# Attention, then two MoE blocks, on one core: all position-bias groups ahead of the attention loop, engines in hand-written order, and a full-height last key chunk

## The chip, the cores and the metric

The kernel runs as one program on 1 core of one Trainium2 chip. The metric is the device time of one execution in microseconds, as the median of several runs. The engines are TensorE (PE in the profile, PEld for its weight loads), VectorE (DVE), ScalarE (ACT), GpSimd (POOL) and SyncE (SP), which here only issues DMAs.

## The reference, cut to what matters

Attention with a learned position bias, then two feed-forward blocks. Everything is float32.

```
B, H, S, D = 4, 8, 576, 64
scores = q @ k.T / sqrt(D)
psi    = log1p(|i - j|) / log1p(max(i, 1))
bias   = relu(psi * w1 + b1) @ w2              # 32 hidden, then 8 heads
attn   = softmax(scores + bias[None])          # divided by (sum + 1e-9)
x      = attn @ v                              # 2304 tokens x 512
h = x @ w_in;  g = P(h) / (Q(h) + 1e-6);  x = g @ w_out        # 512 -> 2048 -> 512
h = max(x @ w1, x @ w2, x @ w3);          out = h @ w_out2     # 512 -> 768 -> 512
```

The bias depends on the two positions and the head only, so it is computed once for all four batches.

## The kernel before, in words

**Bias.** The 576 rows of the bias are cut into 36 groups of 16 rows: t = 0 to 3 with eight groups each, t = 4 with four. `bias_hidden` makes the hidden layer of one group in four tiles c = 0 to 3 of 128x576: c = 0 on ScalarE (L173), the others on VectorE (L176). `bias_out` multiplies them by w2 on TensorE (L185, PSUM tile `pb`), copies the result out as `bo` on ScalarE (L194; three of the 36 on VectorE, L192) and writes it to HBM with a DMA that ScalarE issues (L197). `bias_load` reads a finished block t back for a pair of heads, issued by SyncE (L204 to L212).

**Attention.** Heads go in pairs p, and a unit is (batch b, block t of 128 query rows, pair p); t = 4 has 64 rows for each of the two heads. There are 80 units, five for each of 16 pairs. In a tick n the loop body `attn_tick` issues the scores of unit n (`scores`, tiles `s`), the softmax of unit n (`reduce_min` on VectorE, `expo` on ScalarE), the reciprocal of unit n-1 (`normalise`: an addition on GpSimd at L269, a reciprocal on VectorE at L270, the broadcast `rb` on GpSimd at L272), the transposes of unit n-2 (`tp`, `tt`, where the last one at L303 transposes `rb`), and a part of a product with v (`attn_v`). `attn_v` runs over five chunks of keys: four of 128 keys as 128x64 tiles of TensorE for each head, and the last 64 keys of each head as a 64x64 tile (L338, `av<-att`). Before a pair can be scored, `split_kq` turns its k and q into high and low float32r parts in six pieces, all on GpSimd (L138 to L153); the loads for that are issued by SyncE ahead of time (`LL`, `SL` are the leads in ticks).

**The first ticks.** The first two pairs of batch 0 run interleaved. After each piece of their `split_kq` two bias groups are issued (`bias_step`), and the first 8 ticks (`NM0`) use the step list `A1`, which holds a bias group at four places. In this part a scheduler sets the order of all engines but SyncE. From tick 8 on the list is `A2`, and SyncE, TensorE and VectorE go in the order of the code (`MAN` 2), while the scheduler still places ScalarE and GpSimd.

**The end of attention.** Weights of the first feed-forward block are turned into high and low parts while the last 19 ticks run (`WT` 61; the low parts of w_in on GpSimd at L408), and x is read back and split from tick 72 on. Then `ffn_tick` and `moe_tick` follow, which the change leaves as they are.

**Buffers.** Most tiles (k, q, v, their parts, bias, `h`, `bo`, `e`, the weights) come from one pool `slot` of 35 buffers of equal size. A new tile takes the buffer of a released one and waits for the last reader of that one, whichever engine or DMA it is.

Of the kernel before, what the change touches and what calls it, by code (L numbers as in the profile page):

```python
# [8 lines left out]
F32 = mybir.dt.float32  # L9
# [20 lines left out]
KN = {'NSLOT': 35, 'NRAW': 3, 'NRAWX': 2, 'NATT': 4, 'HB': 0, 'NE': 'd', 'FP': 2, 'BL': 4, 'T4': 0, 'LSP': 1, 'KX': 4, 'HT': 'ss', 'EVP': 'da', 'TTP': 'dda', 'NXS': 4, 'EARLY': 0, 'NM0': 8, 'MAN': 2, 'MANF': 3, 'A1': ['b', 'T', 'sc', 'st', 'r0', 'av', 'b', 'b', 'b', 'sq', 'n', 'r1', 'p2', 'v0', 'v1', 'e0', 'e1'], 'A2': ['sc', 'av', 'p1', 'T', 'r1', 'r0', 'n', 'st', 'p2', 'sq', 'e0', 'e1', 'v0', 'v1'], 'LL': 10, 'SL': 4, 'LL0': 9, 'SL0': 4, 'SQ': [2, 1, 1], 'CUT2': 2, 'CUT3': 3, 'WS': 9, 'WE': 70, 'WT': 61, 'XT': 8, 'XA': 3, 'XB': 8, 'F': ['g2a', 'g2d', 'h', 'g1a', 'w', 'g2p', 'g1d', 'g1p', 'y', 'x', 'g3'], 'LOW': 4, 'LOM': 3, 'LOI': 0, 'GHI': 'dve', 'GLO': 'dve', 'BED': 8, 'BE0': 16, 'NU1': 'pool', 'XE': ['act', 'pool'], 'WR': 1, 'YSP': 'act', 'LAG': 2, 'EV1': 'dve', 'XSE': 'act', 'STQ': 'sp', 'PUQ': 'sp', 'NB0': 0, 'HP': 0, 'SB': 2, 'XLA': 3, 'XLB': 6, 'XSA': 11, 'YL': 10, 'YS': 14, 'WLOW': 1}  # L30
# [7 lines left out]
def tile_attention_moe(  # L38
# [67 lines left out]

    bias_d = [dr.tile([P if t < 4 else 64, H, S], F32, tag=f"bias{t}", name=f"bias_d{t}") for t in range(5)]
# [21 lines left out]
    def split_kq(b, p):  # L129
# [4 lines left out]
        lo_eng = pool  # L134
        low = slice(64, P)

        def q_hi():
            pool.tensor_scalar(qs, qr[:, :, :512], 1.0, 0.0, ALU.mult, ALU.add)  # L138

        def q_lo(u):  # L140
            lo_eng.tensor_tensor(qs[low, u], qr[low, u, :512], f32(qs[low, u]), ALU.subtract)

        def k_hi(u):
            pool.tensor_scalar(ks[u][:, 0], kr[:, u], 1.0, 0.0, ALU.mult, ALU.add)

        def k_lo(u):
            pool.tensor_tensor(ks[u][:, 1], kr[:, u], f32(ks[u][:, 0]), ALU.subtract)

        def tail(u):
# [4 lines left out]

        return [
            lambda: (q_hi(), k_hi(0)), lambda: (k_lo(0),), lambda: (q_lo(0), k_hi(1)),
            lambda: (k_lo(1),), lambda: (q_lo(1),), lambda: (tail(0), tail(1)),
# [5 lines left out]
    def bias_hidden(t, g):  # L163
        hs = []
        for c in range(4):
# [6 lines left out]
            if c == 0:  # L172
                act.activation(dst, src, AF.Relu, bias=bcol)  # L173
            else:
                on_pool = c == 3 and KN["HP"] and g % KN["HP"] == 0 and (t, g) >= (1, 4)
                (pool if on_pool else dve).tensor_scalar(dst, src, bcol, 0.0, ALU.add, ALU.max)  # L176
# [3 lines left out]
    def bias_out(t, g):  # L180
# [10 lines left out]
        if g % KN["BED"] == 1 and 8 * t + g >= KN["BE0"]:  # L191
            dve.tensor_scalar(bo, pb[:, :, :HS], sc, None, ALU.mult)  # L192
        else:
            act.activation(bo, pb[:, :, :HS], AF.Copy, scale=sc)  # L194
        rows = bias_d[t][g * 16:(g + 1) * 16].rearrange("i h j -> (i h) j")
        bo = bo.rearrange("p x j -> p (x j)")
        act.dma_start(rows, bo)  # L197
# [67 lines left out]

    def normalise(b, t, p):
        et, st = ex[b, t, p]
        r = st[:, 2:4] if t < 4 else st[:, 2:3]
        pool.tensor_scalar(r, r, 1e-9, 0.0, ALU.add, ALU.add)  # L269
# [53 lines left out]
    def attn_v(b, ts, p, js=range(5)):  # L323
# [279 lines left out]
    bnext = [0]  # L603

    def bias_step():
        i = bnext[0]
        if i < len(bgroups):
            if i == 0:
                bias_hidden(*bgroups[0])
            if i + 1 < len(bgroups):  # L610
                bias_hidden(*bgroups[i + 1])
            t, g = bgroups[i]
            bias_out(t, g)
            if g == (7 if t < 4 else 3):
                for p in range(NP):
# [274 lines left out]
```

## Time and profile before

| | us |
|---|---|
| median of 3 runs | 1082.96 (1081.78 to 1083.26) |
| the profiled execution, its own time | 1085.02 |
| its span, first to last instruction | 1083.2 |
| TensorE busy | 1034.7 |
| VectorE, ScalarE, GpSimd busy | 657.7, 622.8, 452.7 |

Busy times are over the whole span; the stages differ. Up to about 100 us the bias is made, attention runs to about 360 us, the first feed-forward block to about 790 us, the second to the end. The granted TensorE clock is 0.982 of full speed on the mean.

### The profile page before, as it was taken

To read this page: it belongs to the slowest core of one execution; us is meant where nothing else is said; L and a number is where in the kernel's file an instruction comes from. 1 tells how busy PE (TensorE), PEld (TensorE's weight loads), DVE (VectorE), ACT (ScalarE), POOL (GpSimd) and SP (SyncE) were. 2 spreads that over 40 slices of the span, in tenths; PEclk is the share of its full clock that TensorE was granted. 3 is DMA by queue.
4 is the path that set the end of the run, shared out by engine and by line. 5 is a ranking of instruction groups with operands and counts; after the bars stand their busy time and mean duration, and the time that the engine had idled before them with its cause. 6 is when DMAs were issued, how large, how long until landed. Compare 5 with 4: busy or idle time off the path is not lost. (4 is left out here: it accounts for less than half of the span.)

```text
span 1083.2 us, 16519 instructions
## 1 busy us (share of the span) xinstructions
PE 1034.7 (96%) x5996; PEld 814.2 (75%) x5996; DVE 657.7 (61%) x1296; ACT 622.8 (57%) x1226; POOL 452.7 (42%) x569
## 2 busy tenths in 40 slices
PE   5689899999998889999999999999999999999998
PEld 2247777777765668878889888788888888888887
DVE  8485667676665789777779877799954211111111
ACT  5685676776776878676678766788733211211111
POOL 7605767677696534332233322333533330211111
PEclk9799999999998889999999999999999999999999
DMA  7486854454453442010020200034243200201010
GB/s 266 138 298 216 294 182 151 158 190 158 157 184 123 147 142 78 1 59 1 0 79 1 79 1 0 24 114 136 84 142 105 78 1 1 78 1 59 1 40 20
DMA packets 43394, 107.94 MB, mean 100 GB/s; under 512 B 4784, under 2 KB 11184, under 8 KB 43312
## 3 DMA queue, kind: packets, MB, share of 16 engines
q1 hardware_dynamic: 38128, 96.27, 26.8%
q10 hardware_dynamic: 5184, 10.62, 2.5%
q8 instruction: 47, 0.77, 0.3%
q14 instruction: 35, 0.29, 0.1%
HBM read 77.90 MB, written 28.97 MB: 99 GB/s over the span
## 5 line engine op out<-in xcount | busy, mean ns | idle before, releaser
L454 PE MATMUL p<-ys,wm 128*128 128x512 f32 (+1 forms) x1080 | 227.0, 368 | 0.0
L454 PE MATMUL ph<-xs,wwi 128*128 128x512 f32 (+1 forms) x960 | 215.9, 373 | 3.5 <-ACT at L743 2.6
L454 PEld LDWEIGHTS p<-ys,wm 128*128 128x128 f32 x1080 | 188.9, 188 | 34.3
L454 PE MATMUL y<-gs,wwo 128*128 128x512 f32 (+1 forms) x905 | 204.4, 373 | 1.3 <-POOL gs L502 1.1
L454 PEld LDWEIGHTS ph<-xs,wwi 128*128 128x128 f32 x960 | 169.7, 190 | 38.4 <-POOL xs L446 3.0
L502 POOL TENSOR_TENSOR gs<-g,gs 128x512 fp32r<-128x512 f32 (+1 forms) x80 | 96.1, 1201 | 237.2 <-ACT gs L501 170.2
L454 PEld LDWEIGHTS y<-gs,wwo 128*128 128x128 f32 x905 | 158.4, 188 | 34.5 <-POOL gs L502 2.4
L264 ACT ACTIVATE e<-e,st 128x576 f32<-128x576 f32 x144 | 111.1, 772 | 61.2 <-DVE st L258 44.3
L258 DVE CUSTOM_DVE_ANT_0 e<-s,bias 128x576 f32<-128x576 f32 x144 | 104.3, 754 | 44.9 <-PE s L233 32.4
L546 POOL TENSOR_TENSOR h2s<-mx,h2s 128x512 fp32r<-128x512 f32 (+1 forms) x30 | 35.5, 1183 | 225.5 <-ACT h2s L545 225.5
L542 DVE TENSOR_TENSOR mx<-p,mx 128x512 f32<-128x512 f32 (+1 forms) x30 | 19.1, 637 | 141.4 <-PE p L454 137.5
L475 ACT ACTIVATE s<-ph,keep 128x512 f32<-128x512 f32 (+1 forms) x80 | 49.5, 618 | 90.3 <-PE ph L454 89.9
L545 ACT CAST h2s<-mx 128x512 fp32r<-128x512 f32 (+1 forms) x30 | 17.3, 578 | 127.8 <-DVE mx L543 127.8
L296 PEld LDWEIGHTS tp<-ident,e 128*128 128x128 f32 x576 | 62.1, 141 | 35.7 <-issue 20.1
L233 PE MATMUL s<-k,qs 128*128 128x288 f32 x512 | 86.4, 309 | 2.2 <-ACT bo L194 1.5
L296 PE MATMUL tp<-ident,e 128*128 128x128 f32 x576 | 81.5, 281 | 1.2 <-ACT at L743 1.2
L477 DVE SCALAR_TENSOR_TENSOR g<-g,keep,s 128x512 f32<-128x512 f32 (+1 forms) x80 | 55.3, 692 | 41.5 <-ACT g L476 40.4
L338 PE MATMUL av<-at,v 128*64 128x320 f32 (+3 forms) x576 | 79.0, 396 | 0.0
L560 PE MATMUL o<-wmo,h2s 128*128 128x512 f32 x324 | 78.6, 390 | 0.0
L233 PEld LDWEIGHTS s<-k,qs 128*128 128x128 f32 x512 | 71.3, 191 | 5.6 <-issue 2.6
L185 PE MATMUL pb<-h,keep 128*32 128x288 f32 x576 | 49.2, 450 | 24.1 <-ACT h L173 23.2
L560 PEld LDWEIGHTS o<-wmo,h2s 128*128 128x128 f32 x324 | 60.4, 188 | 12.6 <-POOL h2s L546 0.4
(98 smaller groups left out, 1599.6 us busy)
## 6 DMA issues: line engine op xcount, KB each, us to landing
bias_d<-bo ACTq DMA_DIRECT2D x36, 288.0 KB, 3.1
kr<-in_k SPq DMA_DIRECT2D x16, 576.0 KB, 4.3
qr<-in_q SPq DMA_DIRECT2D x16, 576.0 KB, 4.3
bias<-bias_d SPq DMA_DIRECT2D x16, 576.0 KB, 5.5
wrm<-in_m SPq DMA_DIRECT2D x18, 512.0 KB, 3.6
wrwin<-in_wi SPq DMA_DIRECT2D x16, 512.0 KB, 5.4
wrwo<-in_wo SPq DMA_DIRECT2D x16, 512.0 KB, 3.6
v<-in_v SPq DMA_DIRECT2D x8, 576.0 KB, 4.3
```

The source lines that it names most:

```text
L185: pe.matmul(pb[32 * c:32 * c + 32, x, :HS], lhsT=hw_sb, rhs=hs[c][:, x * HS:(x + 1) * HS], start=True, stop=True,)
L233: pe.matmul(pt[:, x, :HS], lhsT=qs[:, u, t * P:(t + 1) * P], rhs=ks[u][:, w, x * HS:(x + 1) * HS], start=w == 0, stop=w == 1,)
L258: dve.tensor_tensor_reduce(out=dst, in0=src, in1=bs, op0=ALU.add, op1=ALU.min, scale=-0.125, scalar=3.0e38, accum_out=st[:, u:u + 1],)
L264: act.activation(et[:, u], et[:, u], AF.Exp, bias=st[:, u:u + 1], scale=-1.0, accum_out=st[:, 2 + u:3 + u])
L296: pe.transpose(tp[:, j * P:(j + 1) * P], flat[:, 640 * u + j * P:640 * u + (j + 1) * P], ident)
L338: pe.matmul(po[r, :n], lhsT=l, rhs=m, start=j == 0, stop=j == 4, skip_group_check=True)
L454: pe.matmul(po, lhsT=wpart(key, a, k), rhs=rhs, start=first and i == 0, stop=last and i == 2)
L475: act.activation(s, ph, AF.Abs, scale=B0)
L477: dve.scalar_tensor_tensor(q, q, B1, s, ALU.mult, ALU.add)
L502: pool.tensor_tensor(t[1], u, f32(t[0]), ALU.subtract)
L546: pool.tensor_tensor(t[:, 1], m, f32(t[:, 0]), ALU.subtract)
L560: pe.matmul(po, lhsT=h[:, a, tt * P:(tt + 1) * P], rhs=w[c], start=j == 0 and i == 0, stop=j == NF2 - 1 and i == 2,)
```

## The change

What stays: what is computed, the units and their order, the two feed-forward blocks.

1. `attn_v`: the last key chunk of each head is a 128x64 tile like the others. Its v part lies in a new tile `vz` (three buffers) that has zeros in the other head's 64 rows; GpSimd zeroes it once and copies 64x64 of v per head into it with the last piece of `split_kq` (`v_tail`).
2. All 36 bias groups are issued before the first tick. The list `A1` and the 8 ticks with it are gone.
3. In the bias part the splits of the first two pairs (all but the small `tail` and `v_tail`) go to VectorE, one piece behind each of groups 3 to 14.
4. In eight groups (2, 4, ... 16) the hidden tile c = 1 goes from VectorE to ScalarE as well. All `bo` copies are on ScalarE.
5. The bias stores are issued by SyncE. The bias block of t is loaded three groups after its last group (`BW`).
6. The bias part and all 80 ticks go in the order of the code on all five engines (`MAN` 3).
7. In a tick: the addition before the reciprocal (`sum_guard`) stands first, one split piece stands before the broadcast `rb` and one after it, `r0` before `r1`; the loads stand at the end of the tick.
8. Numbers: loads 7 ticks ahead instead of 10 and splits 4 ahead instead of 6; early weights from tick 12 instead of 9; the late weights from tick 64 instead of 61, with every second low part of w_in on VectorE.

```
-KN: 'NM0': 8, 'MAN': 2, 'LL': 10, 'SL': 4, 'SQ': [2, 1, 1], 'WS': 9, 'WT': 61, 'LOI': 0
+KN: 'NM0': 0, 'MAN': 3, 'LL': 7, 'SL': 3, 'SQ': [1], 'WS': 12, 'WT': 64, 'LOI': 2, 'H2': [2, 4, ... 16], 'SP0': [3, 4], 'BW': 3
...
+    vz = sb.tile([P, 3, 2, 64], F32, tag="vz", name="vz")
+    pool.memset(vz, 0.0)
...
-    def split_kq(b, p):
+    def split_kq(b, p, eng=pool):
...
+        def v_tail():
+            for u in range(2):
+                r = slice(64 * u, 64 * u + 64)
+                pool.tensor_copy(vz[r, (NP * b + p) % 3, u], vv[b, p][r, 512:])
...
-            if c == 0:
+            if c == 0 or c == 1 and 8 * t + g in KN["H2"]:
                 act.activation(dst, src, AF.Relu, bias=bcol)
...
-        act.dma_start(rows, bo)
+        sp.dma_start(rows, bo.rearrange("p x j -> p (x j)"))
...
+    def sum_guard(b, t, p):
+        r = ex[b, t, p][1][:, 2:4 if t < 4 else 3]
+        pool.tensor_scalar(r, r, 1e-9, 0.0, ALU.add, ALU.add)
...
-                    l, m = vt[r, 512:], a2[r, 0, :n]
+                    l, m = vz[:, (NP * b + p) % 3, u], a2[:, 0, :n]
...
+    with ordered(3):
+        todo_at = {}
+        for p in range(KN["FP"]):
+            for n, f_ in enumerate(split_kq(0, p, dve)):
+                todo_at.setdefault(KN["SP0"][p] + 2 * n, []).append(f_)
+        NG = len(bgroups)
+        bias_hidden(*bgroups[0])
+        for i, (t, g) in enumerate(bgroups):
+            if i + 1 < NG:
+                bias_hidden(*bgroups[i + 1])
+            for f_ in todo_at.pop(i, []):
+                f_()
+            bias_out(t, g)
...
-        for step in KN["A1" if n < KN["NM0"] else "A2"]:
+        for step in KN["A2"]:
```

Three places show what moves. **GpSimd at the start of the program**, before; the names are the parts of k and q of pairs 0 and 1 (`qs`, `k`), and `st`, `rb` of the first unit:

```order
L138 TENSOR_SCALAR qs_0_112<-qr_0_104 128x1024
L144 TENSOR_SCALAR k_0_0_113<-kr_0_102 128x576
L152 TENSOR_SCALAR qtail<-qr_0_104 128x64 x2
L141 TENSOR_TENSOR qs_0_112<-qr_0_104,qs_0_112 64x512 x2
L147 TENSOR_TENSOR k_0_0_113<-kr_0_102,k_0_0_113 128x576
L153 TENSOR_TENSOR qtail<-qr_0_104,qtail 64x64 x2
```

And now, with `st`, `rb` of the first unit behind it:

```order
L154 TENSOR_SCALAR qtail<-qr_0_106 128x64
L155 TENSOR_TENSOR qtail<-qr_0_106,qtail 64x64
...
L160 COPY vz<-v_0_112 64x64 x2
L154 TENSOR_SCALAR qtail<-qr_1_110 128x64
L155 TENSOR_TENSOR qtail<-qr_1_110,qtail 64x64
...
L270 TENSOR_SCALAR st_0_0_822<-st_0_0_822 128x2
L277 COPY rb_0_0_855<-st_0_0_822 128x128
```

The wide operations have left GpSimd; the 64-column ones (each head once, so twice the rows shown for `qtail`) and the copies into `vz` are left there.

**ScalarE in the bias part**, before:

```order
L194 ACTIVATE bo_1_156<-pb_1_147,keep 128x576
L173 ACTIVATE h_3_0_160<-tab_sb,psi 128x576
L197 DMA bias_d_93<-bo_1_156 128x576
L194 ACTIVATE bo_2_175<-pb_2_166,keep 128x576
L173 ACTIVATE h_4_0_178<-tab_sb,psi 128x576
L197 DMA bias_d_93<-bo_2_175 128x576
```

And now:

```order
L197 ACTIVATE bo_1_161<-pb_1_152,keep 128x576
L180 ACTIVATE h_3_0_164<-tab_sb,psi 128x576
L197 ACTIVATE bo_2_179<-pb_2_170,keep 128x576
L180 ACTIVATE h_4_0_182<-tab_sb,psi 128x576 x2
L197 ACTIVATE bo_3_199<-pb_3_190,keep 128x576
```

The DMA issues are gone from ScalarE, and group 4 has a second hidden tile there.

**GpSimd late in attention** (batch 3; `rb_4_1` belongs to unit t = 4 of pair 1, `k_3_*` to the split of pair 3, `wwi` are weights of the first feed-forward block), before:

```order
L147 TENSOR_TENSOR k_3_0_4096<-kr_3_3853,k_3_0_4096 128x576
L144 TENSOR_SCALAR k_3_1_4097<-kr_3_3853 128x576
L408 TENSOR_TENSOR wwi_4158<-wrwi_4007,wwi_4158 128x512
L269 TENSOR_SCALAR st_0_2_4113<-st_0_2_4113 128x2
L404 TENSOR_TENSOR wwi_4056<-wrwi_4108,wwi_3848 128x128
...
L272 COPY rb_4_1_4148<-st_4_1_4062 128x128
```

And now:

```order
L413 TENSOR_TENSOR wwi_4119<-wrwi_3967,wwi_4119 128x512
L270 TENSOR_SCALAR st_4_1_4083<-st_4_1_4083 128x1
L277 COPY rb_4_1_4162<-st_4_1_4083 128x128
L280 COPY e_4_1_4082<-e_4_1_4082 128x64
L270 TENSOR_SCALAR st_0_2_4128<-st_0_2_4128 128x2
L140 TENSOR_SCALAR qs_3_4188<-qr_3_4074 128x1024
L146 TENSOR_SCALAR k_3_0_4189<-kr_3_4072 128x576
L277 COPY rb_0_2_4208<-st_0_2_4128 128x128
```

The broadcast `rb_4_1` stood behind pieces of a split and of weights; now it stands right behind the addition to `st` of its unit, and the split begins after it.

## Rows read from the trace of the kernel before

**Rows 1.** The page's first line.
```profile
span 1083.2 us, 16519 instructions
```

**Rows 2.** Windows: stretch, its length, busy us of each engine, clock, DMA share, GB/s.
```profile
21.00:36.00 15.00, 1.50 (x20) 0.62 (x24) 6.52 (x16) 2.01 (x4) 14.50 (x14) 0.61 0.29 101
...
107.00:300.00 193.00, 190.09 (x1414) 142.71 (x1413) 134.65 (x373) 137.43 (x321) 135.16 (x246) 1.00 0.55 184
300.00:356.00 56.00, 49.68 (x349) 35.99 (x349) 31.58 (x90) 40.63 (x96) 43.40 (x66) 0.94 0.48 150
356.00:400.00 44.00, 38.20 (x173) 27.18 (x172) 35.69 (x61) 33.65 (x64) 23.17 (x24) 0.84 0.54 166
400.00:790.00 390.00, 388.31 (x1863) 322.50 (x1862) 322.13 (x510) 285.74 (x527) 134.90 (x114) 1.00 0.14 47
```

**Rows 3.** Timelines, 5 to 36 us: start, us, engine, line, what, [idle before, releaser].
```profile
5.55 21.98 DVE L176 TENSOR_SCALAR h<-tab_sb,psi 128x576 f32<-128x576 f32 x51
...
9.96 18.47 POOL L138 TENSOR_SCALAR qs<-qr 128x1024 fp32r<-128x1024 f32 x1 [6.89 <-DMA qr<-in_q]
...
34.23 0.74 ACT L194 ACTIVATE bo<-pb,keep 128x576 f32<-128x576 f32 x1 [12.99 <-POOL qtail L153]
...
35.68 2.15 PE L185 MATMUL pb<-h,keep 128*32 128x288 f32 x16 [13.21 <-ACT h L173]
```

**Rows 4.** Timeline of ScalarE, bias part.
```profile
5.23 1.44 ACT L173 ACTIVATE h<-tab_sb,psi 128x576 f32<-128x576 f32 x2 [1.88 <-DVE tab_sb L95]
...
10.97 0.74 ACT L194 ACTIVATE bo<-pb,keep 128x576 f32<-128x576 f32 x1 [0.43 <-PE pb L185]
11.61 0.77 ACT L173 ACTIVATE h<-tab_sb,psi 128x576 f32<-128x576 f32 x1
```

**Rows 5.** Groups of instructions: line, engine, what, xcount, busy us, mean ns, idle before.
```profile
L484 DVE TENSOR_TENSOR g<-ph,g 128x512 f32<-128x512 f32 (+1 forms) x80 | 50.8, 635 | 0.0
...
L153 POOL TENSOR_TENSOR qtail<-qr,qtail 64x64 fp32r<-64x64 f32 x32 | 10.2, 335 | 1.5
...
L152 POOL TENSOR_SCALAR qtail<-qr 128x64 fp32r<-128x64 f32 x32 | 7.2, 244 | 13.9 <-DMA qr<-in_q 13.8
```

**Rows 6.** DMA issues of the bias stores: count, KB each, us to landing.
```profile
bias_d<-bo ACTq DMA_DIRECT2D x36, 288.0 KB, 3.1
```

**Rows 7.** A window late in the bias part; columns as in rows 2.
```profile
50.00:60.00 10.00, 8.97 (x104) 3.70 (x99) 9.08 (x22) 8.68 (x13) 0.00 (x0) 1.00 0.95 318
```

**Rows 8.** Timeline of TensorE, attention.
```profile
196.66 1.30 PE L233 MATMUL s<-k,qs 128*128 128x288 f32 x8
...
213.69 1.30 PE L233 MATMUL s<-k,qs 128*128 128x288 f32 x8
...
359.66 1.95 PE L338 MATMUL av<-at,v 128*64 128x256 f32 x16
361.54 0.65 PE L338 MATMUL av<-att,v 64*64 64x256 f32 x4
362.12 1.09 PE L296 MATMUL tp<-ident,e 128*128 128x128 f32 x8
```

**Rows 9.** Timeline of TensorE: units 9 and 79, and a late wait.
```profile
107.60 1.53 PE L243 MATMUL s<-k,qtail 128*128 128x512 f32 x8
...
329.71 0.48 PE L303 MATMUL tt<-ident,rb 128*128 128x128 f32 x1 [4.68 <-POOL rb L272]
...
356.27 1.53 PE L243 MATMUL s<-k,qtail 128*128 128x512 f32 x8
```

**Rows 10.** Waits of TensorE from 107 to 356 us: us in total, times, longest.
```profile
PE tt L303 <- POOL rb L272: 7.8, 3, 4.7
```

**Rows 11.** Groups of instructions, conversion of w_out weights on VectorE.
```profile
L391 DVE SCALAR_TENSOR_TENSOR wrwo<-wrwo 128x512 int32<-128x512 int32 x16 | 13.0, 815 | 0.7 <-ACT wrwo L382 0.6
...
L383 DVE TENSOR_SCALAR wrwo<-wrwo 128x512 int32<-128x512 int32 x16 | 7.5, 472 | 4.1 <-DMA wrwo<-in_wo 4.1
```

More of the change, by code (lines that the diff above doesn't have):

```diff
@@ L171, in bias_hidden @@
             bcol = psi_sb[:, i0 // 4:i0 // 4 + 1]
-            if c == 0:
+            if c == 0 or c == 1 and 8 * t + g in KN["H2"]:
                 act.activation(dst, src, AF.Relu, bias=bcol)
             else:
-                on_pool = c == 3 and KN["HP"] and g % KN["HP"] == 0 and (t, g) >= (1, 4)
-                (pool if on_pool else dve).tensor_scalar(dst, src, bcol, 0.0, ALU.add, ALU.max)
+                dve.tensor_scalar(dst, src, bcol, 0.0, ALU.add, ALU.max)
             hs.append(dst)
@@ L602, in tile_attention_moe @@
     bgroups = [(t, g) for t in ((4, 0, 1, 2, 3) if KN["T4"] else range(5)) for g in range(8 if t < 4 else 4)]
[L603 to L615, printed above, removed]
-                    if not late(t, p):
-                        bias_load(t, p)
-            bnext[0] += 1
     slim = {"wi": wi, "wo": wo}
@@ L636, in wo_todo, with ordered @@
         return src, "wo", f, f < 11, low_eng(KN['LOW'], f)
+    def ordered(m):
+        names = ["SP", "PE", "DVE", "Pool", "Activation"][:(1, 2, 3, 5)[m]]
+        return tc.manual_schedule(engines={getattr(mybir.EngineType, e) for e in names})
     sqq = []
     load_kq(0, 0)
+    load_kq(0, 1)
     load_v(0, 0)
-    load_kq(0, 1)
-    for p in range(2, KN["FP"]):
-        if p == 2:
-            load_v(0, 2)
-        load_kq(0, p)
-    for p in range(KN["FP"]):
-        for n, f_ in enumerate(split_kq(0, p)):
-            if p >= 2 and KN["LSP"]:
-                sqq.append(f_)
-            else:
-                f_()
-                for _ in range(KN["SB"] if p < 2 else 0):
-                    bias_step()
+    with ordered(3):
[9 more added lines that the diff above has]
+            for f_ in todo_at.pop(i, []):
+                f_()
+            bias_out(t, g)
+            if g == (7 if t < 4 else 3):
+                todo_at.setdefault(min(i + KN["BW"], NG), []).extend(
+                    lambda t=t, p=p: bias_load(t, p) for p in range(NP) if not late(t, p)
+                )
+        for f_ in todo_at.pop(NG, []):
+            f_()
+        assert not todo_at
     NB = len(blocks)
@@ L717, in attn_tick @@
                 bias_load(t, p)
-        for b, p in loads_at.get(n, []):
-            if p % 2 == 0:
-                load_v(b, p)
-            load_kq(b, p)
         u0 = units[n] if n < NU else None
@@ L739, in attn_tick @@
                 ev = transposes(u2[0], u2[2], u2[3])
+            elif step == "na" and u1:
+                sum_guard(u1[0], u1[2], u1[3])
             elif step == "n" and u1:
@@ L747, in attn_tick @@
                 evac(KN["TTP"][n % len(KN["TTP"])], ev[-1])
-            elif step == "b":
-                bias_step()
             elif step in ("p1", "p2"):
@@ L762, in attn_tick @@
                     avq.extend((av, range(sum(cut[:k]), sum(cut[:k + 1]))) for k in range(len(cut)))
-            elif step == "sq":
+            elif step == "sq1":
                 for bp in splits_at.get(n, []):
                     sqq.extend(split_kq(*bp))
-                for _ in range(2 if n < 10 else KN["SQ"][n % len(KN["SQ"])]):
+                if sqq:
+                    sqq.pop(0)()
+            elif step == "sq":
+                for _ in range(KN["SQ"][n % len(KN["SQ"])]):
                     if sqq:
                         sqq.pop(0)()
+        for b, p in loads_at.get(n, []):
+            if p % 2 == 0:
+                load_v(b, p)
+            load_kq(b, p)
         WT, XT = KN["WT"], KN["XT"]
@@ L781, in attn_tick @@
                     split_x("x", 0, kc)
-    def ordered(m):
-        names = ["SP", "PE", "DVE", "Pool", "Activation"][:(1, 2, 3, 5)[m]]
-        return tc.manual_schedule(engines={getattr(mybir.EngineType, e) for e in names})
-    for n in range(KN["NM0"]):
-        attn_tick(n)
     with ordered(KN["MAN"]):
```

20 lines of the change are left out of this document (7 added, 13 removed).

## Prediction

> **What bounds the kernel now.** I read the windows first, then the timelines of the engines in the windows where TensorE is not full. From 400 to 790 us TensorE is busy for 388.3 of 390 us [rows 2], and the last stage is like it; nothing of the change lies there. From 107 to 300 us, in attention, it is busy for 190.1 of 193 us at full clock. So the end is set by TensorE almost everywhere, and what can be won lies in three places before 400 us: the bias part, the stretch 300 to 356 us (49.7 of 56 us busy, mean clock 0.94) and the start of the first feed-forward block, 356 to 400 us (38.2 of 44 us, clock 0.84).
>
> In the bias part one event stands out: between 21 and 36 us TensorE has 1.5 us of work [rows 2]. The timelines [rows 3] show how it came. VectorE made 51 hidden tiles in one run from 5.55 to 27.53 us. GpSimd began its first wide split at 9.96 us and ended it after 18.47 us, 0.9 us after that run ended. The rest of the splits then followed, and ScalarE waited 12.99 us for GpSimd: its next `bo` wanted a buffer of the pool that GpSimd's `qtail` operations still read. TensorE, one step behind, waited 13.21 us.
>
> In attention TensorE needs 17.03 us for five units (scores at 196.66 and 213.69 us, [rows 8]), 3.41 us each. From unit 9 at 107.60 us to unit 79 at 356.27 us [rows 9] there are 70 units: 248.7 us, where 14 times 17.03 is 238.4. The 10.3 us between are waits and the slow clock after them; most of it are three waits for the broadcast `rb` on GpSimd, 7.8 us [rows 10], the longest 4.68 us at 329.71 us [rows 9].
>
> **The change, part by part.** I count from four times: when attention starts, unit 9, unit 79, the end.
>
> Bias part. ScalarE has the most work in it. Two hidden tiles in a row take 1.44 us, one alone 0.77, so the step is 0.67; from `bo` to the next hidden tile it is 0.64 [rows 4]. From the second `bo` at 10.97 us there remain 35 `bo`, 33 tiles c = 0 and 8 extra c = 1: 35 x 0.64 + 41 x 0.67 = 49.9 us, so the last `bo` ends at 60.9 us. VectorE has 100 hidden tiles at 21.98/51 = 0.43 us [rows 3], and the splits: for each pair one operation of 1024 columns and two of 576 of the hidden tile's kind (0.76 + 2 x 0.43 by columns), and tensor-tensor ones, two of 576 and two of 512 columns, at 635 ns for 512 [rows 5] (2 x 0.71 + 2 x 0.64): 4.3 us, 8.6 for both, 51.6 us from 5.55 us on, so it ends at 57 us. The splits thus lie beside ScalarE; without that cover they would cost 8.6. The stores leave ScalarE; on SyncE they queue in front of the bias loads, which in turn wait for a whole block of stores. Nobody needs these loads before unit 0 of their block, tens of us later.
>
> What stays on GpSimd are eight `qtail` operations, four at 244 and four at 335 ns [rows 5], and four copies, about the first kind: 3.3 us. If they wait as the wide one did, they run only once VectorE stops, and the hidden tile that gets their buffer (group 19, by the order) waits for them. The trace of before has no such short operation under a full VectorE run; bounds are 0 (they slip in between) and 13.2 us (the stall as it was). I take 2.8, the part of the 3.3 that the two buffers need, since what is left behind VectorE is now short.
>
> The page of the Trainium skill on this is SBUF — State Buffer, section Who interferes with whom: GpSimd and a VectorE instruction in its two-port mode lock each other out, and the second waits until the first has finished. The 18.47 us [rows 3] agree with the lock but not with a wait for one instruction: they span about 41. By the page each short operation would wait for one hidden tile, 0.43 us, and be long done at group 19. Taken alone that makes the term 0 instead of 2.8.
>
> Attention can start when the last two `bo` free their PSUM tiles: 60.2 + 2.8 = 63 us. Before, units 0 to 8 ran among the bias groups and unit 9 came at 107.60. Now units 0 to 9 run back to back: nine steps at 3.41 are 30.7, less 2 x (3.41 - 1.30) because the first two ticks only have scores (1.30, [rows 8]), plus 1 us to fill the softmax chain: 27.5. Unit 9 at 90.5 us, 17.1 earlier.
>
> Last key chunk. 16 records of 128x64 tiles take 1.88 us from 359.66 to 361.54 us, 0.47 for four; the four records of the 64x64 tiles beside them 0.58, to 362.12 [rows 8]. The 64x64 pair costs more than the full-height one will: 0.1 us for each of the products with 256 columns, one in five units. I count nothing for the other widths. Five units then take 16.93, 14 times 237.0. The copies into `vz`, two of 0.24 us for a pair in 17 us, lie on GpSimd beside TensorE, which is used 135 of 193 us [rows 2]; at the worst they belong to the `rb` wait below.
>
> Order by hand. GpSimd has per tick an addition, up to two split pieces and the broadcast; `rb` of unit n-1 is issued in tick n and used at the end of tick n+1. Behind it now stands at most one piece, not a row of pieces and weights, and every second low part of w_in goes to VectorE, busy 31.6 of 56 us where those lie [rows 2]. So the 7.8 us of waits should mostly go. Other waits can come: five engines in fixed order, a bias load four ticks ahead of its use as before, loads seven ticks ahead. Waits and slow clock from unit 9 to 79 were 10.3 us; I bound them by 0 and 12 and take 6, since half of the heavy load is left. Unit 79 at 90.5 + 237.0 + 6 = 333.5 us, 22.8 earlier than 356.27.
>
> Start of the feed-forward block. Its order on TensorE is the same, but the weights start three ticks later, so three w_out conversions more fall into it: 0.82 + 0.47 us each on VectorE [rows 11], 3.9 us on an engine that is busy for 35.7 of 44 us there [rows 2]. Bounds 0 and 4, I take 3. From then on the work is the same, and a start 19.8 us earlier is an end 19.8 us earlier.
>
> Against its own time: the profiled run took 1085.02 us with a span of 1083.2 [rows 1]; the median is 1082.96, 0.2% below, and I take the gain from that: 1063.
>
> **The rivals.** First, **the stall comes back** in the bias part: GpSimd's short operations starve as the wide one did, and 13.2 us instead of 2.8 pass. For it: the same run of VectorE, longer now. Against: what GpSimd then has to do is 3 us, not 16. 1073.
>
> Second, **the DMA sets the bias part**. 36 stores of 288 KB [rows 6] are 10.6 MB; eight bias loads and five k, q, v loads of 128x1152 floats are 7.7 MB. 18.3 MB at the 318 GB/s of 50 to 60 us, where the DMA share was 0.95 [rows 7], take 58 us, hardly less than ScalarE. A tenth less rate, and the pool's buffers come free late: attention starts at 70 us, 1070.
>
> Third, **GpSimd in fixed order holds TensorE once in each pair**: a split piece that waits for its k or q now stands in front of `rb`, where a scheduler had placed it. This ends on the other side. The three waits of before are 2.6 us on the mean [rows 10]; 14 pairs with one each are 36.4 us in place of the 6, so 30 us later: 1093. It decides from 25.8/14 = 1.8 us for each pair. Against it: per five units GpSimd used 135/193 of its time, and `rb` has a full tick of slack. At just about 1.8 us the gain is eaten and nothing changes.
>
> Fourth, **the short operations slip through**, as by the page, and the term is 0: 1060.
>
> Fifth, the change does not do what it says in one part: zeros in half of the rows cost as much as the 64x64 mode, 1.4 us in all: 1065.
>
> **How the numbers follow.** Forecast 1063: 51%; fourth 13%; fifth 5%; the stall 12%; the DMA 7%; third, slower, 8%; gain eaten, within 0.2%, 4%. A measurement tells 0.2%, 2.2 us, from no change. So faster 0.88, same 0.04, slower 0.08. The range: upwards 7 us for a start at 70, 6 for the waits at 12, 1 for the feed-forward start make 1077; downwards 2.8, 6 and 3 make 1051. Not all come together: 1052 to 1076, which holds all but the slower and the unchanged case and the tips of the others.
>
> **What would show it.** The last `bo` of the bias between 60 and 66 us and no wait of ScalarE over 4 us in it; unit 9 near 90 us, unit 79 near 333; a single form of `av` on TensorE; few waits of TensorE for `rb`. I would be wrong if the last `bo` came after 70 us, or if between units 9 and 79 more than 12 us over 237 passed, with GpSimd's `rb` or ScalarE's copies as the releaser.

## The result, and the profile after

The changed kernel takes 1068.02 us (median of 4 runs, 1066.84 to 1069.53), the kernel before 1082.93 (1081.78 to 1083.26): a ratio of 0.9852, 95% interval 0.9838 to 0.9867. That is 14.9 us faster, where 19.9 were forecast. The time lies in the range, 5 us above the number. The profiled execution of the changed kernel took 1066.84 us. (Of c5, the best kernel below, one of four executions ran at a mean clock of 0.754 and took 1262.66 us; its median and its comparison below leave that one out.)

The first line of its page, and then its windows (stretch, its length, busy us and number of instructions of TensorE, its weight loads, VectorE, ScalarE, GpSimd, then clock, DMA share, GB/s). The first two stretches are those of [rows 2]; the third holds the 56 us in front of unit 79, as 300 to 356 us did before:

```profile
span 1064.9 us, 16574 instructions
```

```profile
21.00:36.00 15.00, 13.38 (x144) 4.24 (x142) 14.81 (x32) 14.78 (x23) 0.00 (x0) 1.00 0.74 253
107.00:300.00 193.00, 189.75 (x1408) 142.63 (x1407) 137.75 (x373) 135.09 (x319) 141.27 (x267) 1.00 0.53 178
283.50:339.50 56.00, 48.17 (x350) 34.96 (x349) 33.71 (x95) 37.93 (x91) 36.48 (x65) 1.00 0.45 148
```

The hole between 21 and 36 us is filled: 13.4 us of TensorE where there were 1.5. But the 56 us in front of unit 79 hold as much work as before, 350 instructions of TensorE where there were 349, so nothing was gained there, and that is the stretch in which the waits were to go. Its TensorE is busy for 48.2 us at full clock, where it was busy for 49.7 at a mean clock of 0.94. The units show where the gain lies. TensorE's timeline of the changed kernel, the scores of unit 9, of two units in the middle, and of unit 79:

```profile
91.59 0.82 PE L245 MATMUL s<-k,qtail 128*128 128x512 f32 x3
...
262.15 1.16 PE L245 MATMUL s<-k,qtail 128*128 128x512 f32 x5
...
279.04 1.17 PE L245 MATMUL s<-k,qtail 128*128 128x512 f32 x5
...
339.46 0.82 PE L245 MATMUL s<-k,qtail 128*128 128x512 f32 x3
```

Against [rows 9]:

| stretch of the span | before, us | after, us | gain forecast | gain in the traces |
|---|---|---|---|---|
| start to unit 9 | 107.60 | 91.59 | 17.1 | 16.0 |
| unit 9 to unit 79 | 248.67 | 247.87 | 5.7 | 0.8 |
| unit 79 to the end | 726.9 | 725.4 | -3 | 1.5 |
| the whole span | 1083.2 | 1064.9 | 19.8 | 18.3 |

The traces differ by 18.3 us and the medians by 14.9, because the profiled execution of before was 2.1 us slower than its median and that of after 1.2 us faster. The mean clocks of the four executions of after were 0.997, 0.994, 0.992 and 0.992, with times of 1066.84, 1067.74, 1069.53 and 1068.30 us.

Three views tell the rest. ScalarE at the end of the bias part, back to back up to the last two `bo` (the starts at 58.31 and 61.04 us are two groups apart):

```profile
58.31 0.74 ACT L197 ACTIVATE bo<-pb,keep 128x576 f32<-128x576 f32 x1
58.95 0.76 ACT L180 ACTIVATE h<-tab_sb,psi 128x576 f32<-128x576 f32 x1
59.62 0.73 ACT L197 ACTIVATE bo<-pb,keep 128x576 f32<-128x576 f32 x1
60.24 0.77 ACT L180 ACTIVATE h<-tab_sb,psi 128x576 f32<-128x576 f32 x1
61.04 0.74 ACT L197 ACTIVATE bo<-pb,keep 128x576 f32<-128x576 f32 x1
62.31 0.74 ACT L197 ACTIVATE bo<-pb,keep 128x576 f32<-128x576 f32 x1 [0.53 <-PE pb L191]
```

GpSimd in the bias part: the first of the small pieces, the second, the last, and then the first addition of attention:

```profile
9.72 2.56 POOL L154 TENSOR_SCALAR qtail<-qr 128x64 fp32r<-128x64 f32 x1 [6.34 <-DMA qr<-in_q]
12.37 0.42 POOL L155 TENSOR_TENSOR qtail<-qr,qtail 64x64 fp32r<-64x64 f32 x1
...
17.00 0.78 POOL L160 COPY vz<-v 64x64 f32<-64x64 f32 x2
65.76 0.24 POOL L270 TENSOR_SCALAR st<-st 128x2 f32<-128x2 f32 x1 [47.98 <-ACT e L266]
```

The first piece took 2.56 us, the others 0.3 to 0.85 for one or two, and from 17.8 us on GpSimd had nothing left to do. Third, the waits (us in total, times, longest): of TensorE from 91 to 340 us, then of VectorE, GpSimd and ScalarE from 300 to 346 us, and last of VectorE in the kernel before from 300 to 356 us:

```profile
PE av L343 <- ACT at L741: 6.7, 8, 2.2
PE s L235 <- DVE st L260: 2.2, 3, 0.9
PE tt L307 <- DVE at L322: 1.5, 1, 1.5
PE tp L301 <- DVE xs L349: 0.7, 1, 0.7
```

```profile
DVE st L275 <- POOL st L270: 18.1, 8, 5.0
...
POOL wwi L413 <- ACT wwi L412: 5.0, 4, 2.4
...
ACT e L266 <- DVE st L260: 14.2, 4, 5.1
```

```profile
DVE st L270 <- POOL st L269: 5.6, 4, 2.9
```

The waits for `rb` of [rows 10] are gone, every one of them. In their place TensorE waits for copies of ScalarE and VectorE. About half of these, as a1 will show, go back to one line: VectorE waits for GpSimd's addition in front of its reciprocal, 18.1 us in 46 (5.6 us in 56 in the kernel before). One such wait, followed through GpSimd, VectorE, TensorE and ScalarE:

```profile
296.56 1.29 POOL L413 TENSOR_TENSOR wwi<-wrwi,wwi 128x512 fp32r<-128x512 f32 x1
297.94 0.22 POOL L270 TENSOR_SCALAR st<-st 128x2 f32<-128x2 f32 x1
...
298.20 0.17 DVE L275 RECIPROCAL st<-st 128x2 f32<-128x2 f32 x1 [3.43 <-POOL st L270]
298.28 1.79 DVE L396 SCALAR_TENSOR_TENSOR wnwin<-wrwin 128x512 int32<-128x512 int32 x1
299.99 0.68 DVE L322 COPY at<-tp 128x512 f32<-128x512 f32 x1
...
300.72 0.33 PE L307 MATMUL tt<-ident,e 128*128 128x128 f32 x1 [1.54 <-DVE at L322]
...
302.17 0.78 ACT L266 ACTIVATE e<-e,st 128x576 f32<-128x576 f32 x1 [5.06 <-DVE st L260]
```

GpSimd's addition of a few columns (0.22 us) stands behind a low part of weights (`wwi`). VectorE goes in written order, so the reciprocal holds its copies and `reduce_min`; a conversion of weights between them (L396) took 1.79 us here beside GpSimd, where its kind takes 0.95 at the median. TensorE and ScalarE then wait for the copies and `reduce_min`. Later low parts on GpSimd wait in turn for a cast of ScalarE (5.0 us in four waits above), which stands behind the exponentials. Engines in fixed order make a ring here, in which each waits for the next. Rival three had GpSimd in fixed order as the holder, but by way of `rb` and split pieces.

### The profile page after: what moved, and what is told of

The parts are those of the page before. It is cut to its first block, busy times and chain, and to the rows that moved or that the text cites. A ratio compares the mean times of both kernels' runs of the same rounds, so it can differ in the third digit from the quotient of the medians.

```text
span 1064.9 us, 16574 instructions
## 1 busy us (share of the span) xinstructions
PE 1025.4 (96%) x5996; PEld 809.9 (76%) x5996; DVE 662.9 (62%) x1307; ACT 627.5 (59%) x1237; POOL 419.9 (39%) x580
## 5 line engine op out<-in xcount | busy, mean ns | idle before, releaser
L550 ACT CAST h2s<-mx 128x512 fp32r<-128x512 f32 (+1 forms) x30 | 17.3, 578 | 127.4 <-DVE mx L548 127.4
L343 PE MATMUL av<-at,v 128*64 128x320 f32 (+3 forms) x576 | 76.7, 390 | 8.6 <-ACT at L741 6.7
L482 DVE SCALAR_TENSOR_TENSOR g<-g,keep,s 128x512 f32<-128x512 f32 (+1 forms) x80 | 55.3, 691 | 36.3 <-ACT g L481 34.9
L494 DVE SCALAR_TENSOR_TENSOR g<-g,keep,s 128x512 f32<-128x512 f32 (+1 forms) x80 | 55.5, 694 | 17.9 <-ACT s L488 14.7
```

Of the source, the lines that this page charges most:

```text
L343: pe.matmul(po[r, :n], lhsT=l, rhs=m, start=j == 0, stop=j == 4, skip_group_check=True)
L482: dve.scalar_tensor_tensor(q, q, B1, s, ALU.mult, ALU.add)
L494: dve.scalar_tensor_tensor(u, u, A0, s, ALU.add, ALU.mult)
```

## The experiments

The kernels named a are the changed kernel with edits, b is the kernel before with one, c are combinations. The ratios are against the kernel before on the same chip. Its medians there were 1084.46 to 1084.60 us, some 1.6 above the 1082.93 of the result, so differences in us from the changed kernel, taken from the medians, are good to about 2 us. Places in the trace, like unit 79, are those of one execution.

**Addition on VectorE (a1).** 

```
-  pool.tensor_scalar(r, r, 1e-9, 0.0, ALU.add, ALU.add)      # step 'na' first in the tick
+  dve.tensor_scalar(r, r, 1e-9, 0.0, ALU.add, ALU.add)       # step 'na' right ahead of 'n'
```

> The changed kernel with one edit: the addition of 1e-9 ahead of the reciprocal is made by VectorE, right in front of its reciprocal, instead of by GpSimd. Theory A: late in attention VectorE, which goes in written order, stands at the reciprocal because the addition on GpSimd queues behind low parts of weights, which wait for ScalarE; 18.1 us of VectorE's idle time from 300 to 346 us and most of TensorE's 9.7 us of waits in the last two pairs come from that. Then these waits go, unit 79 comes some 8 us earlier (331 to 333 us instead of 339.5), and the time falls by 5 to 9 us to about 1060. Rival B: GpSimd has too much to do there, whoever makes the addition; then the broadcast rb becomes late instead, TensorE waits for it as in the kernel before, unit 79 stays within 2 us and the time within 0.2% of the changed kernel's 1068.

Measured: 1062.85 us, ratio 0.9795 (0.9768 to 0.9821). Unit 79 comes at 334.06 us, from unit 9 (93.47 us) it is 240.6 us instead of 247.9. The longest of VectorE's waits, 300 to 346 us; those for GpSimd are gone:

```profile
DVE wwi L413 <- ACT wwi L412: 8.2, 6, 3.0
```

Theory A holds, with less than it named: the queue in front of one small operation cost 7.3 us between units 9 and 79. TensorE waited 0.2 us for `rb` from 296 to 340 us, so GpSimd's sum of work was not it. But the undisturbed five units take 16.89 us, and the last two pairs took 9.7 us more than twice that in the changed kernel and 5.6 here; the other 3.1 us were gained before unit 69, where VectorE had waited for the addition as well (in the changed kernel from 91 to 200 us):

```profile
DVE st L275 <- POOL st L270: 13.9, 14, 2.4
```

What is left in the last two pairs lies beside VectorE's own waits for casts, the first line above; c5 takes those away. Unit 9 was 1.9 us later than in the changed kernel in this execution, behind a wait for `rb` that the loads of pair 2 cause; a8 and c1 move these.

**Low parts on VectorE (a2).** 

```
-'LOI': 2
+'LOI': 1
```

> The changed kernel with every low part of w_in on VectorE instead of every second one (eight operations of 1.28 us leave GpSimd, eight of 0.68 us come to VectorE). Theory A (additions on GpSimd stand behind these low parts): part of the late waits goes, unit 79 comes 3 to 6 us earlier, the time falls by 2 to 5 us. Rival B (GpSimd's sum of work): the same direction. Rival C (the waits come from VectorE or ScalarE being full, not from GpSimd): VectorE gets 5.4 us more and the time grows by up to 5 us. Together with the run that moves the addition this tells queueing behind one operation from load.

Measured: 1068.42 us, ratio 0.9847 (0.9821 to 0.9874), no change. From 296 to 340 us VectorE's waits for the addition fall from 18.1 to 3.0 us, but its waits for ScalarE's casts at the low parts come to 9.3 us in their place: the same ring by another member. Unit 79 comes at 342.41 us, no earlier. A and B expected a gain, and C a loss by load; none of the three came. The reading left is that an operation that waits for ScalarE stands in front of `reduce_min`, whichever engine it is on; this run alone doesn't show it, and c5 bears it out.

**The 64x64 last chunk (a3).** 

```
-  l, m = vz[:, (NP * b + p) % 3, u], a2[:, 0, :n]
+  l, m = vt[r, 512:], a2[r, 0, :n]
```

> The changed kernel with the last key chunk of each head as a 64x64 tile again, as before (the copies into vz stay and are not read). Theory: the full-height chunk is worth what the steps of five undisturbed units show, 16.90 us with it and 17.03 without, 0.13 us for each of 16 pairs, so the time grows by about 2 us (0.2%). Rival: tiles of other widths cost too, up to 4 us. Rival: no difference, the 0.13 us come from elsewhere, and an undisturbed five units still take 16.90 us.

Measured: 1068.12 us, ratio 0.9848 (0.9816 to 0.9881): no difference from the changed kernel, but an interval of 0.3% either way can't tell the 2 us of the theory. The steps can. Its timeline of TensorE shows five undisturbed units:

```profile
263.15 1.17 PE L245 MATMUL s<-k,qtail 128*128 128x512 f32 x5
...
280.18 1.17 PE L245 MATMUL s<-k,qtail 128*128 128x512 f32 x5
```

17.03 us, where the changed kernel takes 16.89 (262.15 to 279.04 above). The gain for a pair is real, and it doesn't reach the end. Unit 9 comes 0.32 us later than in the changed kernel. By unit 69 the delay is 1.3 us (297.22 against 295.94); the last two pairs, which wait for other engines, give most of it back, and unit 79 comes at 339.81 us, 0.35 us later.

**Splits of the first pairs on GpSimd (a4).** 

```
-  for n, f_ in enumerate(split_kq(0, p, dve)):
+  for n, f_ in enumerate(split_kq(0, p, pool)):
```

> The changed kernel with the splits of the first two pairs on GpSimd, as before the change, in the same places of the written order. Theory: wide GpSimd operations starve beside VectorE's run of hidden tiles, and the buffers that they read hold up the bias part: ScalarE waits 10 to 15 us in it, the last bo ends at 73 to 78 us instead of 62.96, and the time grows by 9 to 14 us to 1077 to 1082. Rival: what had stalled the kernel before was its interleaved order and not the splits; then with all 36 groups in one row GpSimd catches up in time, the last bo ends within 3 us of 63 and the time stays within 0.3%.

Measured: 1072.76 us (1067.79 to 1073.46), ratio 0.9876 (0.9842 to 0.991). The wide operation does starve, but the last `bo` starts at 64.27 us, 1.96 us later, and behind its first `bo` ScalarE never waits over 1 us. Timelines of GpSimd, and of TensorE near 87 us:

```profile
9.64 10.26 POOL L140 TENSOR_SCALAR qs<-qr 128x1024 fp32r<-128x1024 f32 x1 [6.27 <-DMA qr<-in_q]
...
87.31 0.33 PE L308 MATMUL tt<-ident,rb 128*128 128x128 f32 x1 [2.72 <-POOL rb L277]
87.39 1.30 PE L235 MATMUL s<-k,qs 128*128 128x288 f32 x8
89.49 2.26 PE L343 MATMUL av<-at,v 128*64 128x128 f32 x15 [0.80 <-DVE xs L349]
```

The theory named a stall of 10 to 15 us, and it didn't come back; the rival holds for the bias part, while the time grew by 0.2 to 0.4%, at the edge of its 0.3%. VectorE ran out of buffers after 31 tiles, at 19.00 us, and the wide operation ended 0.9 us later. Unit 9 comes at 98.68 us, 7.1 later. Behind the bias part this execution has a wait of 2.72 us that ends at 87.31 us and a clock that fell behind it (0.79 in 80 to 96 us, 1.00 in the changed kernel).

**The kernel before, with the splits on VectorE (b1).** 

```
+  eng = dve if b == 0 and p < 2 else pool                    # in split_kq
...
-  pool.tensor_scalar(qs, qr[:, :, :512], 1.0, 0.0, ALU.mult, ALU.add)
+  eng.tensor_scalar(qs, qr[:, :, :512], 1.0, 0.0, ALU.mult, ALU.add)   # the other pieces too, all but tail
...
```

> The kernel before the change with one part of the change alone: the splits of the first two pairs (but the qtail pieces) on VectorE instead of GpSimd; interleaved first ticks, scheduler and all else as before. Theory of the prediction: the wide GpSimd operations that starve beside VectorE's run are the stall; then TensorE's wait of 13.2 us near 36 us shrinks to under 3 us, unit 9 comes at 94 to 100 us instead of 107.6 and the time falls by 7 to 13 us against the kernel before. Rival, from the run with the splits back on GpSimd in the changed kernel, where the bias part ended only 2 us later: the stall belongs to the interleaved order, in which VectorE runs 51 tiles ahead; then with the splits on VectorE a wait of over 6 us stays in the first 60 us and unit 9 comes after 102 us.

Measured: 1076.59 us, ratio 0.9921 (0.9898 to 0.9945): 7.9 us faster. The wait of 13.2 us is gone: no wait of over 1 us is left to TensorE between 12 and 60 us. Unit 9 comes at 100.94 us, just past the 94 to 100 of the theory. A new wait stands at the start, where the first split on VectorE waits 4.49 us for its load and hidden tiles stand behind it:

```profile
11.34 8.31 PE L185 MATMUL pb<-h,keep 128*32 128x288 f32 x62 [4.46 <-DVE h L176]
```

So the stall of [rows 3] was the wide split on GpSimd, as the prediction read it. Together with a4: in the old order moving the splits cures it, and in the new order it would hardly have come.

**Stores issued by ScalarE (a5).** 

```
-  sp.dma_start(rows, bo.rearrange("p x j -> p (x j)"))
+  act.dma_start(rows, bo.rearrange("p x j -> p (x j)"))
```

> The changed kernel with the bias stores issued by ScalarE again, as before the change. Theory of the prediction: where SyncE issues them they cost nothing, and on ScalarE, which bounds the bias part, each issue costs what stands between its operations; the last bo ends 1 to 4 us later than 62.96 us for the 36 issues, and the time grows by as much. Rival: an issue takes no time of ScalarE that shows (bo to hidden tile was 0.64 us before and is 0.63 now); the last bo ends within 0.5 us, and the time changes only by what the loads on SyncE gain, which then no longer stand behind stores: up to 2 us less.

Measured: 1079.23 us, ratio 0.9943 (0.9928 to 0.9958), 11 us lost. ScalarE (ACT for its work, ACTq for its DMA issues):

```profile
57.51 0.72 ACT L197 ACTIVATE bo<-pb,keep 128x576 f32<-128x576 f32 x1
58.26 0.33 ACTq L199 DMA_DIRECT2D bias_d<-bo  x1
58.63 0.78 ACT L180 ACTIVATE h<-tab_sb,psi 128x576 f32<-128x576 f32 x1 [0.40 <-ACT bo L197]
59.32 0.72 ACT L197 ACTIVATE bo<-pb,keep 128x576 f32<-128x576 f32 x1
```

Neither expectation was large enough. The issue waits for the end of its own `bo` and holds the next hidden tile by 0.40 us; a group takes 1.81 us instead of 1.37, and the last `bo` starts at 76.99 us, 14.7 us later. In the kernel before, the scheduler had put the next hidden tile between `bo` and its issue (the order of ScalarE before, shown with the change), and there `bo` to hidden tile was 0.64 us [rows 4]. So the move to SyncE is what lets the written order of ScalarE run at this pace.

**ScalarE and GpSimd placed by the scheduler in the ticks (a6).** 

```
-'MAN': 3
+'MAN': 2
```

> The changed kernel with a scheduler placing ScalarE and GpSimd in the 80 ticks, as before the change (SyncE, TensorE and VectorE stay in written order, the bias part too). Theory A: the written order of these two engines took the waits for rb away and brought the waits of VectorE for the addition; without it rb waits of 5 to 8 us come back in the last pairs and the waits of VectorE for the addition fall under 8 us, so the time stays within 4 us of 1068. Theory B: the written order is what gains in attention; then unit 9 to unit 79 takes 4 us or more longer and the time is over 1072. Theory C: the written order costs; then unit 79 comes 5 us earlier and the time is under 1064.

Measured: 1091.52 us, ratio 1.006 (1.0037 to 1.0084): slower than the kernel before. Waits of TensorE, 63 to 366 us:

```profile
PE tt L308 <- POOL rb L277: 28.4, 8, 8.0
```

Theory B holds, with 23 us where it named 4 or more. Unit 9 comes at 99.82 us, 8.2 later, behind the longest of these waits, and from there to unit 79 it is 265.2 us, 17.3 longer. With the new steps and loads the scheduler puts `rb` behind other work of GpSimd, up to 8.0 us late. With this list of steps the written order is worth that much. It isn't its gain over the kernel before, whose scheduler and older list took 248.7 us from unit 9 to unit 79, 0.8 more than the changed kernel.

**Weights two ticks earlier (a7).** 

```
-'WT': 64
+'WT': 62
```

> The changed kernel with the late weights of the first feed-forward block starting at tick 62 instead of 64 (tick 61, as before the change, can't be built). Theory of the prediction: each tick of delay leaves about 1 us of conversions in the start of the block; then the stretch from unit 79 to the end (725.4 us in the changed kernel) shrinks by 2 us, and two more ticks in attention have weights. Rival, from the runs so far, in which this stretch was shorter the later unit 79 came (721.9 us at 365.0, 728.8 at 329.2): the weights take a fixed time from their start, and what attention waits for them is given back in the block; then unit 79 comes 1 to 3 us later, the stretch is that much shorter, and the time stays within 1 us of 1068.

Measured: 1076.31 us (1073.1 to 1078.04), ratio 0.9914 (0.9893 to 0.9935): 7 to 8 us slower than the changed kernel. Unit 79 comes at 343.48 us, 4.0 later, and the stretch behind it takes 730.9 us, 5.5 longer instead of shorter. Both expectations fall. VectorE's waits for the addition from 296 to 345 us, here and then in the changed kernel:

```profile
DVE st L275 <- POOL st L270: 21.4, 8, 4.9
```

```profile
DVE st L275 <- POOL st L270: 21.5, 9, 5.0
```

They are the same, so the 4.0 us are not more of this wait. TensorE's waits from 279 us to unit 79 sum to 9.5 us instead of 7.9, and the clock is 0.97 in 295 to 345 us, where the changed kernel kept 1.00 from 296 to 340. Why the start of the block is longer too is not settled: TensorE's waits from 345 to 420 us sum to 10.4 us (8.3 from 341 to 420 us in the changed kernel), and the clock from 300 to 400 us is 0.93 instead of 0.98.

**Loads of pair 2 ahead of the bias loads of t = 4 (a8).** 

```
-  loads_at.setdefault(i - lead, []).append((b, p))
+  if (b, p) != (0, 2):
+      loads_at.setdefault(i - lead, []).append((b, p))
...
+  load_v(0, 2)
+  load_kq(0, 2)
   for f_ in todo_at.pop(NG, []):
```

> The changed kernel with one edit: the loads of v, k and q of pair 2 are issued right behind the last bias store, ahead of the bias loads of block t = 4, which wait for these stores to land (in the changed kernel they are issued at 72.6 to 73.8 us, behind them, and GpSimd waits 5.35 us for q, to 80.83 us; TensorE then waits near 83 us). Theory: the loads go out at some 66 us, that wait of GpSimd falls under 1.5 us, TensorE has no wait and no slow clock between 80 and 96 us, unit 9 comes at 90.0 to 90.6 us in place of 91.59, and the time falls by 1 to 4 us, with less spread, since the other runs of the changed kernel were longer with a lower mean clock. Rival: the first wait for rb or xs there is ScalarE's or VectorE's doing, then unit 9 stays within 0.5 us and the time within 1 us.

Measured: 1064.04 us (1063.63 to 1065.85), ratio 0.9812 (0.9794 to 0.983), some 4 us better than the changed kernel. GpSimd's first split in attention and TensorE's scores of unit 9, and then that split in the changed kernel:

```profile
76.17 1.05 POOL L140 TENSOR_SCALAR qs<-qr 128x1024 fp32r<-128x1024 f32 x1 [0.69 <-PE s L235]
...
89.65 0.82 PE L245 MATMUL s<-k,qtail 128*128 128x512 f32 x3
```

```profile
80.83 1.05 POOL L140 TENSOR_SCALAR qs<-qr 128x1024 fp32r<-128x1024 f32 x1 [5.35 <-DMA qr<-in_q]
```

The theory holds: unit 9 is 1.94 us earlier. In the changed kernel the loads stood on SyncE behind bias loads that wait for the last stores, were issued at 72.57 to 73.75 us, and GpSimd began this split at 80.83 us. But unit 79 comes at 338.61 us, only 0.85 earlier, and the two traces end 0.9 us apart: from unit 9 to unit 79 this kernel takes 1.1 us more, so about half of the gain is lost again. With the addition on VectorE it arrives in full (c1). The traces thus show 0.9 of the 4 us of the median. The changed kernel was traced in its fastest execution and a8 in its slowest. A lower clock in the others of the changed kernel would fit (means of 0.992 to 0.994, and 0.996 to 0.998 in those of a8), since the waits that end at 84.53 us in a1 and 87.31 us in a4 were each followed by a stretch at about 0.58 of full speed, but those executions left no trace.

**Both edits (c1), and two more on top (c5, c2).** c1 is a1 with a8.

> The changed kernel with both edits: the addition ahead of the reciprocal on VectorE, and the loads of pair 2 ahead of the bias loads of t = 4. If the two waits are independent, as their places (80 to 90 and 296 to 340 us) say, the gains add: unit 9 at 90.3, unit 79 at about 331, and a time of 1058 to 1061, 2 to 4 us under the kernel with the addition on VectorE alone (1062.9). If the wait at 84 us only moves, no gain over that one.

Measured: 1060.30 us, ratio 0.9771 (0.9748 to 0.9794), as expected of independent gains, 2.6 us under a1: unit 9 at 89.63 and unit 79 at 329.20 us, 3.8 and 4.9 us earlier than there. c5 is c1 with `'LOI': 0`, all low parts of w_in on GpSimd:

> The changed kernel with the addition on VectorE, the loads of pair 2 ahead of the bias loads of t = 4, and in addition every low part of w_in on GpSimd (as before the change) instead of every second one. In the kernel with the first two edits VectorE still waits for ScalarE's casts at its low parts, in front of reduce_min, in 300 to 340 us, and unit 79 stands at 329.2 us where 14 undisturbed steps would bring it to about 323. Theory: with no weights on VectorE there these waits go, unit 79 comes 3 to 6 us earlier and the time falls by 2 to 5 us to 1055 to 1058. Rival: GpSimd's broadcast rb then queues behind the low parts, which wait for the same casts, TensorE waits for rb by over 3 us in 296 to 340 us and the time stays within 2 us of 1060 or grows.

Measured: ratio 0.9708 (0.969 to 0.9726), 1053.28 us, 14.7 us under the changed kernel and the fastest of all. TensorE's waits from 91 to 340 us, and unit 79:

```profile
PE av L343 <- ACT at L744: 1.5, 3, 0.7
PE tt L308 <- POOL rb L277: 1.1, 2, 0.9
```

```profile
326.51 0.82 PE L245 MATMUL s<-k,qtail 128*128 128x512 f32 x3
```

With nothing on VectorE that waits for a cast in these ticks, unit 9 (89.44 us) to unit 79 takes 237.1 us, and the last two pairs exceed twice 16.89 by 2.2 us (9.7 in the changed kernel, 4.8 in c1). The low parts on GpSimd wait for casts there too (2.8 us from 296 to 340 us), but now `rb`, which has a tick of slack, stands behind them and not the addition. c2 is c1 with the step list ending in `'v0', 'v1', 'e0', 'e1'`:

> The changed kernel with the addition on VectorE, the loads of pair 2 ahead of the bias loads of t = 4, and in each tick the copies of the transposes (v0, v1) ahead of the exponentials (e0, e1) on ScalarE. Theory: TensorE's remaining waits for ScalarE's copy at (0.75 us near 96, 0.7 near 303, 1.2 near 323, 3.2 near 344 us) shrink to under half and the time falls by 1 to 4 us. Rival: the exponentials come later by the wait for the transposes, and with them the sums and rb; then TensorE waits for rb or for transposes of e instead, and the time grows by 2 us or more.

Measured: 1056.51 us (1054.88 to 1058.18), ratio 0.973 (0.9713 to 0.9747), 3.8 us better than c1. TensorE's waits for ScalarE's copies in attention fall to 0.2 us. The 2.9 us near 344 us stay, and new ones for `reduce_min`, 2.4 us, come. c5 and c2 together were not tried.

## Why the prediction came out as it did

The time lies near the forecast because of the start: 16.0 us were gained up to unit 9, where 17.1 were forecast. Attention gave 0.8 us instead of 5.7, and the loss of 3 us behind it didn't show, which hides part of that miss. So the mechanism held for the start and failed for the order by hand, and that the sum came within 5 us is in part luck.

**Bias part: right in sum, by two errors, which is luck.** ScalarE sets it, as forecast, and VectorE with all splits is done at 58.3 us. But the term of 2.8 us for GpSimd's short pieces was nothing: they were done at 17.8 us, and the hidden tile that was to wait for them waited for no one. In exchange ScalarE's arithmetic was too low. The step of two groups was 2.73 us, not 2 x 1.31, and the last `bo` ended at 63.05 us, not at 60.9. First scores came at 62.17 us against 63. Rival four, short operations slip through, had the mechanism right, and the gain it named was eaten by the ScalarE term. How the 16.0 us divide was not separated in full: in the old order the splits on VectorE alone bring unit 9 forward by 6.7 us (b1), and the eight tiles moved to ScalarE and the groups ahead of the loop had no run of their own.

The page of the Trainium skill on this, SBUF — State Buffer, section Who interferes with whom, said that the second engine waits until the first has finished. The short pieces here bear it out better than the wide one did, though the first of them (2.56 us) waited for more than one tile of 0.43 us, and the wide operation of a4 took 10.26 us.

**What the stores cost was counted at nothing, and that was right only for SyncE.** The prediction took 0.64 us from `bo` to hidden tile from a row in which the scheduler had hidden the issue. Run a5 shows what a written order with the issue on ScalarE would have made of it: 14.7 us.

**Unit 9: 91.59 instead of 90.5 us.** The 27.5 us from the start of attention were right where nothing waits: in a8 from 62.14 to 89.65 us they are 27.5. The 1.9 us more in the changed kernel are the late loads of pair 2. "Loads seven ticks ahead" was named as a possible wait, but the queue that they stand in on SyncE, behind loads that wait for stores, was not followed.

**Last key chunk: right for a pair, worth less in the sum.** 0.14 us for five units (0.1 forecast), which makes 2.0 over 14 steps (1.4 forecast); from a3, 0.35 us arrive at unit 79, no more than stood at unit 9, since the last pairs wait for other engines anyway.

**Order by hand: the step that failed.** 6 us of waits were taken between units 9 and 79, and there were 14.5. The sum shows 247.87 - 237.0 = 10.9, but 237.0 was too high: the first of the 14 steps has fewer products with v to do than the others and takes 14.82 us with a wait of 1.02 us in it, so 13 x 16.89 + 13.8 = 233.4 us are the undisturbed length, and 247.9 less that is 14.5, 9.7 of them in the last two pairs. The waits for `rb` went, as forecast. What was missed is the edge from GpSimd's addition to VectorE's reciprocal. The prediction named what is queued behind GpSimd's pieces (`rb`), but not what is queued behind the reciprocal on VectorE, which a written order holds up with it. The trace of before had the sign, in a row that the prediction did not take up: VectorE waited 5.6 us for the addition from 300 to 356 us. Moving the addition (a1) gives 7.3 us of this stretch back, and with the low parts off VectorE and the loads moved too (c5) it is 237.1 us.

**Start of the feed-forward block: the loss didn't show.** 3 us were forecast, and the traces show a gain of 1.5. But with the weights from tick 64 this stretch took 721.9 (a6) to 728.8 us (c1) in the traces here, and the 726.9 of before lies between, so neither sign stands. Run a7 puts the weights two ticks earlier and makes that stretch 5.5 us longer. That a later start of the weights leaves more conversions to the block is true by count, but no run shows that they set its length; what does is open.

**The rivals.** The stall didn't come back and DMA didn't set the bias part: the last `bo` ended at 63.05 us, though the loads of pair 2 behind the stores were late. The third rival happened in part: the holder is GpSimd in fixed order, but in the last two pairs above all and not once in each, and for 8.5 us more than the 6 taken, not 30. The fifth, zeros as dear as the 64x64 mode, is refuted by the steps of a3.

## What to carry to other kernels

When engines go in written order, look at every small operation that one engine does for another and ask what stands in front of it there and what stands behind its reader: additions of 0.22 us on GpSimd held VectorE for 18.1 us in 46. Move such an operation to its reader's engine (5 us here), and put operations that wait for a distant cast where only work with slack stands behind them (7 us, c1 to c5). A load queued behind loads that wait for stores is as late as these stores; move it ahead of them (4 us alone, 2.6 behind a1). Count an issue of a DMA on the bounding engine by where it stands in its order: hidden behind the next operation it showed no cost, right behind its producer 0.40 us each time.

## What the runs showed of the hardware

How long a GpSimd operation of a given size takes beside VectorE varied widely: 18.47 us for 1024 columns in [rows 3], 10.26 us in a4, 1.05 us in attention; for 64 columns 2.56 and 0.33 us in the same bias part. The two longest ended 0.9 us behind the end of VectorE's run of hidden tiles (51 tiles in [rows 3], 31 in a4), and the 2.56 us 1.1 behind a run of 13. The other way round it shows too: in c1 the addition on VectorE, of one or two columns, took 143 ns at the least, 165 at the median and 1222 at the most. Of the 80, the 22 that took over 0.3 us all ran beside an operation of GpSimd and ended with it, like the longest:

```profile
201.41 1.22 DVE L270 TENSOR_SCALAR st<-st 128x2 f32<-128x2 f32 x1
...
201.34 1.28 POOL L143 TENSOR_TENSOR qs<-qr,qs 64x512 fp32r<-64x512 f32 x1
```

In a4, once GpSimd had its splits under way, VectorE's hidden tiles took 1.42 us each at the median (20.4 to 31 us), and 0.51 in the run of [rows 3].

The clock: behind a wait of TensorE of 1.90 us in a1 the granted clock was 0.58 from 84 to 88 us (eight records of scores in 2.27 us instead of 1.30), and behind waits of 2.72 and 0.80 us in a4 it was 0.59 and 0.56 from 88 to 96 us, near the lower of its two levels, 1.2 of 2.4 GHz. The changed kernel with waits of 0.31 and 0.80 us in the same place kept full clock. It doesn't always fall: a2 had waits of 2.03 and 0.81 us there and kept it too.
